# A Fourier-mixing layer with gated MLP: the first DFT block loaded in halves, two scratch tiles for mod's columns, first products regrouped

## The chip, the cores and the metric

The kernel runs on one core of a Trainium2 chip, a single program on core 0. The metric is the device time of one execution in microseconds (us), the median of several runs. The core's engines work side by side, each through its own instructions in program order: TensorE (PE in the profile) multiplies matrices, VectorE (DVE) and ScalarE (ACT) work element by element, GpSimd (POOL) does small arithmetic and issues some DMAs, SyncE (SP) issues the others.

## The reference

The layer has one sequence x of 2048 rows and 512 columns in 32-bit floats. Cut to what matters:

```
mod = (silu(c) @ w_mod).reshape(1, 6, 1, 512)        # sa, ca, ga, sb, cb, gb
h   = layernorm(x) * (1 + ca) + sa
a   = h @ dft_hid_re.T ;  b = h @ dft_hid_im.T       # 512 x 512
x   = x + ga * (dft_seq_re @ a - dft_seq_im @ b)     # 2048 x 2048
h   = layernorm(x) * (1 + cb) + sb
z   = gelu(h @ w_in)                                 # 512 x 1792, two halves z1, z2
g   = w_sp @ layernorm(z2) + b_sp                    # w_sp 2048 x 2048
x   = x + gb * ((z1 * g) @ w_out)                    # 896 x 512
```

## The kernel before, in words

Every product is made in three: a 32-bit operand is split into a high part (a rounded copy, on ScalarE) and a low part (what is left, on VectorE), and TensorE accumulates high by high, high by low and low by high (`matmul3`, lines 84 to 86). The kernel reorders the first layer: it multiplies the sequence DFT with the normalized x first (`gp`, in `mm_a`), then the result with the hidden DFT (`yp`), into which mod's scale `ca` and shift `sa` have been folded. Column 0 of the normalized x is set to 1 for that.

**Chunks.** The sequence DFT is walked in 512 x 512 blocks of the real and the imaginary matrix. `load_block` brings a block to a `stage` tile by four DMAs on SyncE's queue (line 139); there are two such tiles. A block is four chunks. For each chunk n VectorE transposes 32 x 32 squares into `t` (line 147, `prep_hi`), ScalarE rounds it to `ah` (line 170), and VectorE subtracts for `al` (line 179, `prep_lo`). Of every 128 columns of the block, the first 32 make its first chunk, the next 32 its second, and so on. Then TensorE runs the chunk's twelve matmuls: four column groups of x by three products.

**What sets the order.** The loop over n first makes `t` and `ah` for chunk n + 3 and `al` for chunk n + 2, then runs the matmuls of chunk n, then whatever `at(n, ...)` has put on a list for that chunk. In this way an order written out by hand says in which chunk's part of each engine's queue a piece of side work stands. There are four `ah` and three `al` buffers.

**Side work in the first 32 chunks.** The 16 tiles of x are loaded in groups of four (`load_x`), normalized and split into `hh` and `hl`. For the first eight the statistics are made by VectorE (`stats_x`: lines 92 and 94) and a chain of three GpSimd operations (lines 96, 97, 104); for the other eight by two ScalarE passes with an accumulated sum (`sum_x`, `square_x`) and GpSimd operations. `norm_x` applies them on ScalarE (line 108), then sets column 0, for the first four tiles on ScalarE, else on GpSimd. `hi_h` and `lo_h` split.

mod's `ca` (j = 1) and `sa` (j = 0) are wanted as columns. `load_columns` loads a 512 x 512 piece of w_mod, and for each of its four column groups k `weigh_column` transposes squares into a scratch tile `wt` and multiplies by silu(c), both on VectorE, and `sum_column` sums it on ScalarE in the next chunk's list (line 247). `wt` has one buffer. The hidden DFT's rows are turned later into `ht` tiles by `turn_ht`, the first of them in the tile `y` of the pool `rows`, which otherwise belongs to the post-processing of the `yp` products.

**The start.** SyncE loads two x tiles, the first block, two more x tiles, the second block, two x tiles. Meanwhile TensorE multiplies a constant tile (`keep_busy`), seven matmuls of 32-bit operands, shown as two passes each. Within chunk 0 TensorE goes column group by column group: for each, `hh` by `ah`, `hh` by `al`, `hl` by `ah`.

**After chunk 32.** Three more groups of 32 chunks (t = 1, 2, 3) make the next rows. Between their chunks stand the products `yp` with the hidden DFT for rows of the group before (`mm_y`), each followed by a post-processing on VectorE (`post_y`, `norm_y`, `post_h`). After the last chunk of a half (16 chunks) the four accumulators are split into `gh` and `gl` (lines 80, 81). The two later stages, the gated MLP, are not touched by the change.

Of the kernel before, what the change touches and what calls it, by code (L numbers as in the profile page):

```python
# [19 lines left out]
def fnet_gmlp_kernel(  # L20
# [24 lines left out]
    nc = tc.nc  # L45
    S, D = x.shape[1:]
# [11 lines left out]
    def pool(name, side="left", bufs=1):  # L58
        return tc.tile_pool(name=name, bufs=bufs, side=side, reuse_waits="tile")
# [6 lines left out]
    blocks = ctx.enter_context(pool("blocks"))  # L66
# [4 lines left out]
    def bank(k, name):  # L71
        return psum.tile([P, 512], F32, tag=f"bank{k}", bufs=1, name=name)
# [5 lines left out]
    def split(hi, lo, src):  # L78

        nc.scalar.activation(hi, src, AF.Copy)  # L80
        nc.vector.tensor_tensor(lo, src, hi.bitcast(F32), op=ALU.subtract)
# [25 lines left out]
    def apply(dst, src, scale_shift):  # L107
        nc.scalar.activation(dst, src, AF.Identity, bias=scale_shift[1], scale=scale_shift[0])
# [3 lines left out]
    def at(n, f, *a):  # L112
        fill.setdefault(n, []).append((f, a))
# [9 lines left out]
    src = []  # L123
# [4 lines left out]
    N2 = 4 * len(src)  # L128
# [4 lines left out]
    NE = 4 * len(src)  # L133
    stage, T, AH, AL = {}, {}, {}, {}

    def load_block(tile_, a):
        v = a.rearrange("(b j) (a s) -> a j b s", j=32, a=4)
        for q in range(4):
            nc.sync.dma_start(tile_[32 * q:32 * q + 32], v[q])

    def load(b):
        if b < len(src):
            stage[b] = blocks.tile([P, 16, P], F32, tag="stage", bufs=2, name=f"stage{b}")
            load_block(stage[b], src[b])

    def squares(dst, block, k):
        nc.vector.transpose(dst.rearrange("p (b i) -> p b i", i=32), block[:, :, 32 * k:32 * k + 32])  # L147
# [27 lines left out]
    def prep_lo(n):  # L175
        if n >= NE:
            return
        AL[n] = blocks.tile([P, Q], F32R, tag="al", bufs=3, name=f"al{n}")
        nc.vector.tensor_tensor(AL[n], T.pop(n), AH[n].bitcast(F32), op=ALU.subtract)  # L179
# [4 lines left out]
    rows = p2.enter_context(pool("rows", "right"))  # L184
    s1 = ctx.enter_context(ExitStack())
    spool = s1.enter_context(pool("spool", "right"))
# [7 lines left out]
    ones = cpool.tile([P, P], F32, name="ones")  # L194
# [28 lines left out]
    WB, WT, COL = {}, {}, {}  # L223
# [13 lines left out]
        COL[j] = htpool.tile([P, ND], F32, name=f"col{j}")  # L237

    def weigh_column(j, k):
        WT[j, k] = spool.tile([P, D], F32, tag="wt", bufs=1, name=f"wt{j}_{k}")  # L240
        squares(WT[j, k], WB[j], k)
        nc.vector.tensor_tensor(WT[j, k], WT[j, k], WB["c"], op=ALU.mult)

# [11 lines left out]
    def keep_busy(n, k):  # L255

        ps = bank(k, "busyp")
        for _ in range(n):
            nc.tensor.matmul(ps, ones, busy, start=True, stop=True)
# [14 lines left out]
    X, XG, LN, NRM, h_hi, h_lo = {}, {}, {}, {}, {}, {}  # L274

    def load_x(g, ks=range(4)):

        if g not in XG:
            XG[g] = spool.tile([P, 4, D], F32, tag="x", bufs=2, name=f"x{g}")
        k0, k1 = ks[0], ks[-1] + 1  # L280
        v = x.rearrange("(g a k i) d -> g a i k d", g=NQ, a=4, i=32)
        for a in range(4):
            nc.sync.dma_start(XG[g][32 * a:32 * a + 32, k0:k1, :], v[g, a][:, k0:k1, :])
        for k in ks:
            X[4 * g + k] = XG[g][:, k, :]
# [17 lines left out]
        NRM[s] = m[:, 2:3], m[:, 3:4]  # L303

    def norm_x(s):
        if s not in LN:
            LN[s] = spool.tile([P, D], F32, tag="xn", bufs=4, name=f"xn{s}")
        apply(LN[s], X.pop(s), NRM.pop(s))
        if s < 4:
            nc.scalar.activation(LN[s][:, 0:1], ones[:, 0:1], AF.Copy)  # L310
        else:
            nc.gpsimd.memset(LN[s][:, 0:1], 1.0)

    def parts_h(s, t):

        return t[s].rearrange("p k (a i) -> p k a i", i=32), LN[s].rearrange("p (a k i) -> p k a i", a=4, i=32)

    def hi_h(s):
        h_hi[s] = hpool.tile([P, ND, P], F32R, name=f"hh{s}")
        nc.scalar.activation(*parts_h(s, h_hi), AF.Copy)  # L320
# [8 lines left out]
    GP, gt_hi, gt_lo, YP = {}, {}, {}, {}  # L329
# [3 lines left out]
    def mm_a(n):  # L333
        t, r = divmod(n, 8 * NQ)
        j, s = ((r // 4) % 2, r // 8 * 4 + r % 4) if t == 0 else (r // NS, r % NS)
        if s == 0:
            for k in range(ND):
                GP[t, j, k] = bank(4 * j + k if t == 0 else ring[0] % 6, f"gp{t}_{j}_{k}")
                ring[0] += t > 0
        ah, al = AH.pop(n), AL.pop(n)  # L340
        for k in range(ND):
            matmul3(GP[t, j, k], h_hi[s][:, k, :], h_lo[s][:, k, :], ah, al, s == 0, s == NS - 1)
        if s == NS - 1:
            for k in range(ND):
# [261 lines left out]


    load_x(0, range(2))
    load(0)
    load_x(0, range(2, 4))  # L610
    load(1)
    load_x(1, range(2))
    keep_busy(7, 5)
    for s in range(2):
        stats_x(s)
    for s in range(2):
        norm_x(s)
    hi_h(0)
    prep_hi(0)
    lo_h(0)  # L620
    prep_lo(0)
    hi_h(1)
    prep_hi(1)
    stats_x(2)
# [12 lines left out]
    at(9, silu_row)  # L637
    at(4, load_x, 2)
    at(5, load_columns, 1)
    at(8, load_columns, 0)  # L640
    at(12, load_x, 3)
    at(19, load_ht, 0)
    at(28, load_ht, 1)
    for s, n in ((4, 4), (5, 4), (6, 6), (7, 6)):
        at(n, stats_x, s)
        at(n + 1, norm_x, s)
        at(n + 2, hi_h, s)
        at(n + 3, lo_h, s)
    for s, n in zip(range(8, NS), (10, 11, 12, 13, 18, 19, 20, 21)):
        at(n, sum_x, s)  # L650
        at(n + 1, square_x, s)
        at(n + 2, norm_x, s)
        at(n + 3, hi_h, s)
        at(n + 4, lo_h, s)
    for j, ns in ((1, (12, 13, 16, 18)), (0, (19, 20, 21, 23))):
        for k, n in enumerate(ns):
            at(n, weigh_column, j, k)
            at(n + 1, sum_column, j, k)
# [6 lines left out]
    ones_r = htpool.tile([P, P], F32R, name="ones_r")  # L665
    at(24, nc.scalar.activation, ones_r, ones, AF.Copy)
    at(26, change_pools)
    for j, turn, weigh, row, fold, hi in ((0, (24, 25, 26, 27), (29, 29, 30, 30), 25, (34, 34, 35, 36), (38, 35, 36, 37)),
                                          (1, (33, 38, 39, 40), (39, 40, 41, 41), 37, (44, 45, 46, 47), (48, 46, 47, 48))):
        for k in range(ND):  # L670
            at(turn[k], turn_ht, j, k)
            at(weigh[k], weigh_ht, j, k)
            at(fold[k], fold_ht, j, k)
        at(row, scale_w0, j)
        at(row + 1, store_w0, j)
        at(row + 5, load_w0, j)
# [14 lines left out]
    for t in range(NQ):  # L691
        n = 8 * NQ * (t + 1)
        for i in range(4):
            y = N2 - 1 if t == NQ - 1 else (54, 56, 58, 60)[i] if t == 0 else n + (8, 10, 12, 14)[i] if t == 1 else n + 1 + 3 * i
            if i < 2:
                at(y - 4, load_xr, t, i)
            if t == 0:
                at((41, 42, 43, 45)[i], mm_y, t, i, (0,))
                at((42, 43, 44, 46)[i], keep_y, t, i)
            at(y, mm_y, t, i, (0, 1) if t else (1,))  # L700
            if t < NQ - 1:
                at(y + 1, post_y, t, i)
                at(y + 2, norm_y, t, i)
                at(y + 3 if t else 71 + i, post_h, t, i)
                if i < 2:
                    at(y + 2 if t else y + 3, load_xr, t, i + 2)
            else:
                if i > 1:
                    at(N2 - 0.25, prep, N2 + i - 2)
                at(N2 - 0.25, post_y, t, i)  # L710
                at(N2 - 0.25, norm_y, t, i)
                at(N2 - 0.25, post_h, t, i)
                if i < 2:
                    at(N2 - 0.25, load_xr, t, i + 2)
# [59 lines left out]
    for t in range(NQ):  # L774
        n = N4 + NS * (t + 1)
# [14 lines left out]
    t = NQ - 1  # L790
# [61 lines left out]
```

## Time and profile before

| | |
|---|---|
| median of three runs | 1002.48 us (1002.38 to 1003.36) |
| the profiled execution | 1002.74 us |
| its span on the core | 1000.9 us |
| TensorE busy | 989.3 us (99%), 4346 matmul passes |
| VectorE, ScalarE, GpSimd busy | 543.6, 315.1, 142.3 us |
| moved by DMA | 115.08 MB, 115 GB/s in the mean |

The profile is one execution, taken by the hardware profiler. A row of the timeline gives start and duration in us, engine, source line, operation, and output<-inputs by the program's names with shapes; in brackets stands the idle time of the engine before the instruction and what ended it. Matmuls are pipelined, so the time from one start to the next is a matmul's cost, not the shown duration. A row of the waits gives the total in us, the number of times and the longest. A row of a window gives, after the stretch and its length, the busy time and instructions of PE, PEld, DVE, ACT and POOL, TensorE's granted clock as a share of full speed, the DMA engines' mean busy share and GB/s. A row of a DMA queue gives packets, MB, and the share of 16 engines' time.

### The profile page before, as it was taken

The numbers are of one execution on the slowest core, as the hardware profiler recorded it, in microseconds if no ns is written. First come the engines' busy times: TensorE is split into PE (matmuls) and PEld (weight loads), VectorE is DVE, ScalarE is ACT, GpSimd is POOL, SyncE is SP. The second block draws the span as 40 slices with busy tenths as digits, with TensorE's granted clock in tenths as the row PEclk, the third lists the DMA queues.
The fourth block names the chain that finished last, engine by engine and source line by source line (L and its number), as shares of the span: only waits on it lengthen the run. The fifth ranks groups of instructions, "written<-read, shape, count | busy, mean of one in ns | idle before, by whom it ended". The sixth has DMA issues, their size and how long they took to land.

```text
span 1000.9 us, 11701 instructions
## 1 busy us (share of the span) xinstructions
PE 989.3 (99%) x4346; PEld 818.9 (82%) x4346; DVE 543.6 (54%) x830; ACT 315.1 (31%) x513; POOL 142.3 (14%) x282
## 2 busy tenths in 40 slices
PE   8998999999999999999999999999999999999998
PEld 5886888888878888888888998888888888888886
DVE  6768957775566546547433576555332622262315
ACT  4666423232132312222543665431111111111101
POOL 2321000112420122004321111102000200020002
PEclk9999999999999999999999999999999999999999
DMA  9993852666435443556553232435225222522131
GB/s 214 215 198 67 167 138 63 158 166 171 126 103 118 93 109 104 117 127 163 189 204 117 43 80 47 116 69 147 70 63 156 55 64 64 158 64 52 43 137 43
DMA packets 149466, 115.08 MB, mean 115 GB/s; under 512 B 7200, under 2 KB 130080, under 8 KB 149408
## 3 DMA queue, kind: packets, MB, share of 16 engines
q1 hardware_dynamic: 142576, 93.87, 40.7%
q0 software_dynamic: 6304, 20.46, 5.8%
q8 instruction: 34, 0.56, 0.2%
q14 instruction: 24, 0.20, 0.1%
q10 hardware_dynamic: 528, 0.00, 0.0%
HBM read 94.37 MB, written 19.93 MB: 114 GB/s over the span
## 4 chain that ended last, share of the span: by engine, by line
PE 94%; DVE 2%; ACT 1%; DMA 1%; issue 1%; SPq 0%; DVEq 0%; ACTq 0%
PE gp L85 11%; PE gp L86 11%; PE gp L84 10%; PE gw L84 10%; PE gw L86 10%; PE gw L85 10%; PE yp L85 3%; PE yp L84 3%; PE yp L86 3%; PE z2p L85 3%; PE z2p L84 3%; PE z2p L86 3%; PE z1p L84 3%; PE z1p L85 3%; PE z1p L86 3%; PE op L86 2%
## 5 line engine op out<-in xcount | busy, mean ns | idle before, releaser
L170 ACT ACTIVATE ah<-t 128x512 fp32r<-128x512 f32 x224 | 141.5, 632 | 535.6 <-PE gw L86 214.9
L179 DVE TENSOR_TENSOR al<-t,ah 128x512 fp32r<-128x512 f32 x224 | 153.1, 683 | 274.6 <-PE gw L85 143.0
L85 PE MATMUL gp<-al,hh 128*128 128x512 f32 x512 | 201.6, 394 | 4.7 <-DVE al L179 4.7
L84 PE MATMUL gp<-ah,hh 128*128 128x512 f32 x512 | 200.8, 392 | 1.7 <-ACT ah L170 1.7
L86 PE MATMUL gp<-ah,hl 128*128 128x512 f32 x512 | 201.1, 393 | 0.0
L86 PE MATMUL gw<-ah,zl 128*128 128x512 f32 x448 | 174.5, 390 | 0.0
L84 PE MATMUL gw<-ah,zh 128*128 128x512 f32 x448 | 174.5, 389 | 0.0
L85 PE MATMUL gw<-al,zh 128*128 128x512 f32 x448 | 174.5, 389 | 0.0
L147 DVE STREAM_TRANSPOSE t<-stage 128x512 f32<-128x512 f32 x208 | 146.4, 704 | 5.6 <-DMA stage<-in_A_dft_seq_re_dram 2.8
L85 PEld LDWEIGHTS gp<-al,hh 128*128 128x128 f32 x512 | 96.8, 189 | 26.5 <-DVE al L179 6.3
L84 PEld LDWEIGHTS gp<-ah,hh 128*128 128x128 f32 x512 | 97.0, 189 | 23.2 <-ACT ah L170 2.5
L86 PEld LDWEIGHTS gp<-ah,hl 128*128 128x128 f32 x512 | 97.0, 189 | 20.8 <-DVE hl L325 0.4
L86 PEld LDWEIGHTS gw<-ah,zl 128*128 128x128 f32 x448 | 84.1, 188 | 17.5
L85 PEld LDWEIGHTS gw<-al,zh 128*128 128x128 f32 x448 | 84.2, 188 | 17.4
L84 PEld LDWEIGHTS gw<-ah,zh 128*128 128x128 f32 x448 | 84.1, 188 | 17.3
L569 POOL TENSOR_TENSOR u<-u,g 128x512 f32<-128x512 f32 x16 | 21.4, 1340 | 336.1 <-DVE g L567 336.1
L85 PE MATMUL yp<-htl,gh 128*128 128x512 f32 x128 | 51.1, 399 | 0.0
L84 PE MATMUL yp<-hth,gh 128*128 128x512 f32 x128 | 50.5, 394 | 0.0
L86 PE MATMUL yp<-hth,gl 128*128 128x512 f32 x128 | 50.2, 392 | 0.0
L85 PE MATMUL z2p<-wil,ah 128*128 128x448 f32 x128 | 46.8, 366 | 0.0
L84 PE MATMUL z2p<-wih,ah 128*128 128x448 f32 x128 | 46.8, 366 | 0.0
L86 PE MATMUL z2p<-wih,al 128*128 128x448 f32 x128 | 46.8, 366 | 0.0
(125 smaller groups left out, 1132.0 us busy)
## 6 DMA issues: line engine op xcount, KB each, us to landing
stage<-in_A_dft_seq_re_dram SPq DMA_DIRECT2D x64, 256.0 KB, 4.8
stage<-in_A_dft_seq_im_dram SPq DMA_DIRECT2D x64, 256.0 KB, 4.7
stage<-in_B_w_sp_dram SPq DMA_DIRECT2D x64, 256.0 KB, 4.9
stage<-h_d SPq DMA_DIRECT2D x32, 256.0 KB, 4.6
z_d<-z POOLq DMA_DIRECT2D x28, 256.0 KB, 5.9
u<-z_d SPq DMA_DIRECT2D x4, 1792.0 KB, 7.9
wm<-in_w_mod_dram SPq DMA_DIRECT2D x16, 256.0 KB, 5.7
xr<-in_A_x_dram POOLq DMA_DIRECT2D x16, 256.0 KB, 3.0
```

The costliest lines, as they stand in the source:

```text
L84: nc.tensor.matmul(acc, ah, bh, start=first, stop=False)
L85: nc.tensor.matmul(acc, ah, bl, start=False, stop=False)
L86: nc.tensor.matmul(acc, al, bh, start=False, stop=last)
L147: nc.vector.transpose(dst.rearrange("p (b i) -> p b i", i=32), block[:, :, 32 * k:32 * k + 32])
L170: nc.scalar.activation(AH[n], T[n], AF.Copy)
L179: nc.vector.tensor_tensor(AL[n], T.pop(n), AH[n].bitcast(F32), op=ALU.subtract)
L569: eng.tensor_tensor(U[t][:, f, :], U[t][:, f, :], g, op=ALU.mult)
```

## The change

Six edits, all in or around the first 32 chunks but for the last:

- The first block is loaded in two halves of its columns, columns 0 to 63 of every 128 first, which are those of chunks 0 and 1, then the x tiles 2 and 3, then the other half. Each half takes four DMAs.
- `wt` of even column groups uses the tile `y` of `rows`, that of odd groups the tile `wt`.
- In chunks 0 to 3 the twelve matmuls are grouped by product: four `hh` by `ah`, four `hh` by `al`, four `hl` by `ah`. The filler has six matmuls instead of seven.
- Column 0 of the normalized x is set on GpSimd for all tiles, ahead of the normalization, which leaves that column out. x tile 1 is normalized after the first chunk's preparation.
- x tiles 8 and 9 get their statistics from VectorE and GpSimd; the tiles 10 to 15 are taken in other chunks, so are mod's column groups and the turned rows of the hidden DFT, and the last x load stands before the second load of mod's columns.
- For t = 1 the `yp` products stand one chunk earlier.

```
-    def load_block(tile_, a):
+    def load_block(tile_, a, s0=0, s1=P):
         v = a.rearrange("(b j) (a s) -> a j b s", j=32, a=4)
         for q in range(4):
-            nc.sync.dma_start(tile_[32 * q:32 * q + 32], v[q])
+            nc.sync.dma_start(tile_[32 * q:32 * q + 32, :, s0:s1], v[q][:, :, s0:s1])
...
     def weigh_column(j, k):
-        WT[j, k] = spool.tile([P, D], F32, tag="wt", bufs=1, name=f"wt{j}_{k}")
+        pl, tag = (spool, "wt") if k % 2 else (rows, "y")
+        WT[j, k] = pl.tile([P, D], F32, tag=tag, bufs=1, name=f"wt{j}_{k}")
...
-        apply(LN[s], X.pop(s), NRM.pop(s))
-        if s < 4:
-            nc.scalar.activation(LN[s][:, 0:1], ones[:, 0:1], AF.Copy)
-        else:
-            nc.gpsimd.memset(LN[s][:, 0:1], 1.0)
+        nc.gpsimd.memset(LN[s][:, 0:1], 1.0)
+        apply(LN[s][:, 1:], X.pop(s)[:, 1:], NRM.pop(s))
...
+        if n < 4:
+            for a, b in ((h_hi[s], ah), (h_hi[s], al), (h_lo[s], ah)):
+                for k in range(ND):
+                    nc.tensor.matmul(GP[0, 0, k], a[:, k, :], b, start=s == 0 and b is ah and a is h_hi[s], stop=False)
+            return
...
-    load(0)
+    stage[0] = blocks.tile([P, 16, P], F32, tag="stage", bufs=2, name="stage0")
+    load_block(stage[0], src[0], 0, P // 2)
     load_x(0, range(2, 4))
+    load_block(stage[0], src[0], P // 2, P)
...
-    keep_busy(7, 5)
+    keep_busy(6, 5)
...
-    at(8, load_columns, 0)
-    at(12, load_x, 3)
+    at(8, load_x, 3)
+    at(12, load_columns, 0)
...
-    for s, n in zip(range(8, NS), (10, 11, 12, 13, 18, 19, 20, 21)):
+    for s, n in zip(range(10, NS), (11, 12, 15, 16, 18, 19)):
...
-    for j, ns in ((1, (12, 13, 16, 18)), (0, (19, 20, 21, 23))):
+    for j, ns in ((1, (12, 14, 17, 18)), (0, (21, 22, 23, 24))):
...
-            y = ... n + (8, 10, 12, 14)[i] if t == 1 ...
+            y = ... n + (7, 9, 11, 13)[i] if t == 1 ...
```

How the change moves instructions is shown at three places. The first is SyncE's queue at the start: x are the tiles of x, stage_120 the first block, the next stage the second. Before:

```order
L283 DMA x_115<-in_A_x_dram 32x2x512 x4
L139 DMA stage_120<-in_A_dft_seq_re_dram 32x16x128 x4
L283 DMA x_115<-in_A_x_dram 32x2x512 x4
L139 DMA stage_129<-in_A_dft_seq_im_dram 32x16x128 x4
L283 DMA x_134<-in_A_x_dram 32x2x512 x4
```

And now:

```order
L284 DMA x_115<-in_A_x_dram 32x2x512 x4
L139 DMA stage_120<-in_A_dft_seq_re_dram 32x16x64 x4
L284 DMA x_115<-in_A_x_dram 32x2x512 x4
L139 DMA stage_120<-in_A_dft_seq_re_dram 32x16x64 x4
L139 DMA stage_133<-in_A_dft_seq_im_dram 32x16x128 x4
L284 DMA x_138<-in_A_x_dram 32x2x512 x4
```

The first block is two groups of four DMAs, each of 64 instead of 128 columns, with the x tiles 2 and 3 between; four DMAs more stand ahead of the second block.

The second is ScalarE's queue around mod's second set of columns (`wt_0` and `wt_1` of j = 0 are summed into col; `ah` heads each chunk). Before:

```order
L170 ACTIVATE ah_848<-t_846 128x512
L320 ACTIVATE hh_864<-xn_764 128x512
L108 ACTIVATE xn_798<-x_590,sums_799 128x512
L299 ACTIVATE xn_835,sums_836<-x_590,sums_836 128x512
L294 ACTIVATE xn_872,sums_873<-x_590 128x512
L247 ACTIVATE wt_1_840,col_491<-wt_1_840 128x512
L170 ACTIVATE ah_882<-t_880 128x512
```

And now:

```order
L170 ACTIVATE ah_897<-t_895 128x512
L319 ACTIVATE hh_915<-xn_831 128x512
L248 ACTIVATE wt_0_892,col_610<-wt_0_892 128x512
L170 ACTIVATE ah_923<-t_921 128x512
L248 ACTIVATE wt_1_918,col_610<-wt_1_918 128x512
L170 ACTIVATE ah_947<-t_945 128x512
```

Before, five instructions stand between two `ah` with the column's sum as the last; now two or one.

VectorE's queue at the same place. Before:

```order
L147 STREAM_TRANSPOSE t_846<-stage_699 128x512
L179 TENSOR_TENSOR al_850<-t_806,ah_808 128x512
L147 STREAM_TRANSPOSE wt_2_877<-wb_486 128x512
L242 TENSOR_TENSOR wt_2_877<-wt_2_877,crow 128x512
L147 STREAM_TRANSPOSE t_880<-stage_699 128x512
```

And now:

```order
L147 STREAM_TRANSPOSE t_921<-stage_714 128x512
L179 TENSOR_TENSOR al_925<-t_895,ah_897 128x512
L324 TENSOR_TENSOR hl_939<-xn_831,hh_915 128x512
L147 STREAM_TRANSPOSE wt_2_942<-wb_605 128x512
L243 TENSOR_TENSOR wt_2_942<-wt_2_942,crow 128x512
L147 STREAM_TRANSPOSE t_945<-stage_714 128x512
```

The order of a chunk is as before, with an `hl` more in it; `wt_2` now lies in the tile `y`, in which `wt_0` was, while `wt_1` lies in the other.

The third is TensorE's first chunk. Before:

```order
L259 MATMUL busyp<-busy,ones 128x512 x7
L84 MATMUL gp_0_0_233<-ah_175,hh_171 128x512
L85 MATMUL gp_0_0_233<-al_179,hh_171 128x512
L86 MATMUL gp_0_0_233<-ah_175,hl_177 128x512
L84 MATMUL gp_0_1_234<-ah_175,hh_171 128x512
```

And now:

```order
L260 MATMUL busyp<-busy,ones 128x512 x6
L343 MATMUL gp_0_0_236<-ah_175,hh_171 128x512
L343 MATMUL gp_0_1_237<-ah_175,hh_171 128x512
L343 MATMUL gp_0_2_238<-ah_175,hh_171 128x512
L343 MATMUL gp_0_3_239<-ah_175,hh_171 128x512
L343 MATMUL gp_0_0_236<-al_179,hh_171 128x512
```

The first matmul that needs `al` was the second of the chunk and is the fifth.

More of the change, by code (lines that the diff above doesn't have):

```diff
@@ L608, in fnet_gmlp_kernel @@
     load_x(0, range(2))
-    load(0)
+    stage[0] = blocks.tile([P, 16, P], F32, tag="stage", bufs=2, name="stage0")
+    load_block(stage[0], src[0], 0, P // 2)
     load_x(0, range(2, 4))
+    load_block(stage[0], src[0], P // 2, P)
     load(1)
     load_x(1, range(2))
-    keep_busy(7, 5)
+    keep_busy(6, 5)
     for s in range(2):
         stats_x(s)
-    for s in range(2):
-        norm_x(s)
+    norm_x(0)
     hi_h(0)
@@ L621, in fnet_gmlp_kernel @@
     prep_lo(0)
+    norm_x(1)
     hi_h(1)
@@ L639, in fnet_gmlp_kernel @@
     at(5, load_columns, 1)
-    at(8, load_columns, 0)
-    at(12, load_x, 3)
+    at(8, load_x, 3)
+    at(12, load_columns, 0)
     at(19, load_ht, 0)
     at(28, load_ht, 1)
-    for s, n in ((4, 4), (5, 4), (6, 6), (7, 6)):
+    for s, n in ((4, 4), (5, 4), (6, 6), (7, 6), (8, 10), (9, 10)):
+        m = n + (s == 9)
         at(n, stats_x, s)
-        at(n + 1, norm_x, s)
-        at(n + 2, hi_h, s)
-        at(n + 3, lo_h, s)
-    for s, n in zip(range(8, NS), (10, 11, 12, 13, 18, 19, 20, 21)):
+        at(m + 1, norm_x, s)
+        at(m + 2, hi_h, s)
+        at(m + 3, lo_h, s)
+    for s, n in zip(range(10, NS), (11, 12, 15, 16, 18, 19)):
         at(n, sum_x, s)
@@ L667, in fnet_gmlp_kernel @@
     at(26, change_pools)
-    for j, turn, weigh, row, fold, hi in ((0, (24, 25, 26, 27), (29, 29, 30, 30), 25, (34, 34, 35, 36), (38, 35, 36, 37)),
+    for j, turn, weigh, row, fold, hi in ((0, (25, 26, 27, 28), (29, 29, 30, 30), 26, (34, 34, 35, 36), (38, 35, 36, 37)),
                                           (1, (33, 38, 39, 40), (39, 40, 41, 41), 37, (44, 45, 46, 47), (48, 46, 47, 48))):
@@ L693, in fnet_gmlp_kernel @@
         for i in range(4):
-            y = N2 - 1 if t == NQ - 1 else (54, 56, 58, 60)[i] if t == 0 else n + (8, 10, 12, 14)[i] if t == 1 else n + 1 + 3 * i
+            y = N2 - 1 if t == NQ - 1 else (54, 56, 58, 60)[i] if t == 0 else n + (7, 9, 11, 13)[i] if t == 1 else n + 1 + 3 * i
             if i < 2:
```

## The prediction

> **What bounds the kernel now.** I read the page's first part, then TensorE's waits over the whole span, then its timeline around the waits, then what VectorE and ScalarE did there.
>
> ```profile
> span 1000.9 us, 11701 instructions
> PE 989.3 (99%) x4346; PEld 818.9 (82%) x4346; DVE 543.6 (54%) x830; ACT 315.1 (31%) x513; POOL 142.3 (14%) x282
> PE gp L85 <- DVE al L179: 4.7, 4, 3.0
> ```
>
> TensorE is busy 99% of the span and no matmul is added or removed. So only its start, its few waits and its clock can move the end: two places hold nearly all of that. The first is seen in the matmuls (start, duration, and in brackets the wait before):
>
> ```profile
> 24.44 0.39 PE L84 MATMUL gp<-ah,hh 128*128 128x512 f32 x1
> ...
> 76.12 0.39 PE L84 MATMUL gp<-ah,hh 128*128 128x512 f32 x1
> 77.66 0.50 PE L85 MATMUL gp<-al,hh 128*128 128x512 f32 x1 [1.15 <-DVE al L179]
> ...
> 80.29 0.39 PE L84 MATMUL gp<-ah,hh 128*128 128x512 f32 x1
> 83.63 0.66 PE L85 MATMUL gp<-al,hh 128*128 128x512 f32 x1 [2.95 <-DVE al L179]
> ...
> 84.83 0.63 PE L84 MATMUL gp<-ah,hh 128*128 128x512 f32 x1
> 85.25 0.63 PE L85 MATMUL gp<-al,hh 128*128 128x512 f32 x1
> ...
> 88.02 0.39 PE L84 MATMUL gp<-ah,hh 128*128 128x512 f32 x1
> ```
>
> A chunk is twelve matmuls. Chunk 4 starts at 24.44 and chunk 23 at 76.12: 2.72 us a chunk, 0.227 us a matmul, without a gap. At that pace chunk 25 would start at 24.44 + 21 x 2.72 = 81.56; it starts at 88.02. So **6.46 us** are lost in chunks 23 and 24: 4.4 in two waits for `al`, and 2.0 because matmuls after the longer wait start 0.42 us apart, at half pace.
>
> Why `al` was late, on VectorE and then on ScalarE:
>
> ```profile
> DVE wt L147 <- ACT wt L247: 11.9, 5, 3.3
> 76.32 0.71 DVE L147 STREAM_TRANSPOSE t<-stage 128x512 f32<-128x512 f32 x1
> 80.94 0.71 DVE L147 STREAM_TRANSPOSE wt<-wb 128x512 f32<-128x512 f32 x1 [3.34 <-ACT wt L247]
> 81.69 0.69 DVE L242 TENSOR_TENSOR wt<-wt,crow 128x512 f32<-128x512 f32 x1
> 82.30 0.70 DVE L147 STREAM_TRANSPOSE t<-stage 128x512 f32<-128x512 f32 x1
> 82.93 0.65 DVE L179 TENSOR_TENSOR al<-t,ah 128x512 fp32r<-128x512 f32 x1
> 83.50 0.68 DVE L325 TENSOR_TENSOR hl<-xn,hh 128x512 fp32r<-128x512 f32 x1
> 77.12 0.63 ACT L170 ACTIVATE ah<-t 128x512 fp32r<-128x512 f32 x1 [2.57 <-DVE t L147]
> 77.66 0.61 ACT L320 ACTIVATE hh<-xn 128x512 fp32r<-128x512 f32 x1
> 78.18 0.80 ACT L108 ACTIVATE xn<-x,sums 128x512 f32<-128x512 f32 x1
> 78.88 0.71 ACT L299 ACTIVATE xn<-x,sums 128x512 f32<-128x512 f32 x1
> 79.59 0.62 ACT L294 ACTIVATE xn<-x 128x512 f32<-128x512 f32 x1
> 80.20 0.61 ACT L247 ACTIVATE wt<-wt 128x512 f32<-128x512 f32 x1
> ```
>
> It is a ring. With one `wt` tile, VectorE may not transpose the next column group until ScalarE has summed the last one. That sum stands last in the ScalarE queue of the same chunk, behind `ah`, `hh` and three passes over x; and `ah` heads that queue waiting for VectorE's `t`. One round takes from `t` at 76.32 to `t` at 82.30, 5.98 us against TensorE's 2.72. Chunks 19, 20 and 21 each carry such a step, so about 3 x 3.26 = 9.8 us fall behind; `al` has three buffers, two chunks (5.4 us) of lead; 9.8 - 5.4 = 4.4 is what TensorE waited.
>
> **The change part by part.**
>
> *Two scratch tiles.* Column group k now waits for the sum of k-2, which stands in an earlier chunk's ScalarE queue. The ring is open unless the queues themselves are too long. From the starts above VectorE spends 0.63 on `t`, 0.57 on `al`, 0.75 + 0.61 on `wt`, and at most its 0.68 on `hl`. In the new order chunks 21 to 24 hold t, al, wt (2.56), t, al, hl, wt (3.24), the same (3.24), and 2.56: 11.6 us for 10.9 us of matmuls. That costs 0.7 of the 5.4 us lead, and TensorE nothing. ScalarE (`ah` 0.54, `hh` 0.52, `xn` 0.70, square 0.71, sum 0.61) holds at most ah, hh, xn, square, sum, at 3.1, in chunks 12 and 13, and 3.0 in 18 and 19, with 1.8 to 2.3 between them. Moving x tiles 8 and 9 to VectorE's statistics adds two pairs to chunk 10: 1.2 + 2 x 0.83 = 2.9 us there, after a chunk of 1.2, and takes 1.3 a tile off ScalarE. So I take the whole 6.46. The bounds: nothing gained if the ring closes elsewhere, and no more than 6.46, since that is all TensorE lost there. If the lead is gone, each microsecond VectorE is late is a microsecond of TensorE.
>
> The even groups borrow the `y` tile, whose next user is the first turned tile of the hidden DFT, at chunk 25. It waits for the sum in ScalarE's chunk 24, again the earlier queue. Cost: nothing, covered by the lead.
>
> *The start.* SyncE's queue, VectorE, GpSimd, ScalarE, TensorE, a window and a DMA queue:
>
> ```profile
> 2.56 2.02 SPq L139 DMA_DIRECT2D stage<-in_A_dft_seq_re_dram  x4
> 5.38 0.69 DVE L92 BATCH_NORM_STATS2 bstx<-x 128x6 f32<-128x512 f32 x1 [4.00 <-DMA x<-in_A_x_dram]
> 9.92 0.71 DVE L147 STREAM_TRANSPOSE t<-stage 128x512 f32<-128x512 f32 x1 [2.83 <-DMA stage<-in_A_dft_seq_re_dram]
> 8.59 0.26 POOL L104 TENSOR_SCALAR nmrx<-mvx,rsx 128x1 f32<-128x1 f32 x1
> 9.84 0.61 ACT L320 ACTIVATE hh<-xn 128x512 fp32r<-128x512 f32 x1
> 10.66 0.63 ACT L170 ACTIVATE ah<-t 128x512 fp32r<-128x512 f32 x1 [0.21 <-DVE t L147]
> 1.53 8.12 PE L259 MATMUL busyp<-busy,ones 128*128 128x512 f32 x14 [1.53 <-DVE busy L201]
> 11.35 0.49 PE L84 MATMUL gp<-ah,hh 128*128 128x512 f32 x1 [1.70 <-ACT ah L170]
> 12.07 0.77 PE L85 MATMUL gp<-al,hh 128*128 128x512 f32 x1 [0.23 <-DVE al L179]
> 14.53 0.71 DVE L147 STREAM_TRANSPOSE t<-stage 128x512 f32<-128x512 f32 x1
> 13.00:14.00 1.00, 1.00 (x4) 0.74 (x3) 0.97 (x4) 0.30 (x1) 0.48 (x1) 0.50 1.23 247
> 19.89 0.61 ACT L320 ACTIVATE hh<-xn 128x512 fp32r<-128x512 f32 x1
> q10 hardware_dynamic: 528, 0.00, 9.7%
> ```
>
> The block lands 9.92 - 5.38 = 4.54 us after the x tiles: 2048 packets of 512 B over 16 engines, 35.5 ns each. Half a block has as many packets, of 256 B, a size this trace does not hold. From both sides: 17.7 ns by bytes, 35.5 if a packet costs what it did, so 2.27 to 4.54 us. The 4-byte packets of c (last row, a window of 3 us: 0.097 x 48 us / 528) cost 8.8 ns, so a small packet is not dear; the straight line between gives 22 ns, a half in 2.84 us. I take that: `t` of chunk 0 can start at 8.2. Then `hh` is last: its column memset stands behind GpSimd's second chain, which ends at 8.59 + 0.26, so `hh` runs 9.0 to 9.6, `ah` to 10.2, and the first matmul starts near 10.3 (before, 0.69 after `ah` began): 1.05 earlier. Chunk 2 needs the second half: 8.2 + 2.3 (x tiles, 512 KB at the block's rate) + 2.84 = 13.4, when VectorE, also 1.05 earlier, comes to it. The next block lands at 17.9, 1.1 later than by bytes, with three chunks of lead, as for every load behind it (`t` is made three chunks ahead). The four DMAs more take 2.0 us of issuing (2.02 for four), while the data of those ahead, 4.54 us a block, still flows: nothing, and at most 2.0 on loads with that lead.
>
> The regrouped products let four matmuls run before `al` is wanted, so the 0.5 us between 11.35 and 12.07 beyond one matmul goes. From 11.35 to 24.44 is 13.09 = 10.88 (four chunks) + 0.50 + 1.71, the last from the half clock that the window's 0.50 shows. If it stays, chunk 4 starts at 10.3 + 10.88 + 1.71 = 22.9: **1.55 us**. Chunk 3's `hh` ended 5.97 after chunk 2's `t` began (14.53 to 20.50): statistics, GpSimd's chain, `xn`, `ah` and itself stand between. So it ends near 19.4, before TensorE comes at 20.2. Bounds: at 35.5 ns a packet the second half lands at 9.92 + 2.3 + 4.54 = 16.8, chunk 3's `hh` ends at 22.7 and chunk 4 starts at 25.4, 1.0 lost; without the half clock `hh` sets chunk 3 at 19.4 and chunk 4 at 22.1, 2.3 gained.
>
> [...]
>
> *The shift of t = 1's y by one chunk.* One wait of 0.4 us is left, where four `gl` meet the post-processing of a y:
>
> ```profile
> PE gp L85 <- DVE al L179: 0.4, 1, 0.4
> ...
> 284.25 2.76 DVE L81 TENSOR_TENSOR gl<-gp,gh 128x512 fp32r<-128x512 f32 x4 [6.40 <-ACT gh L80]
> 287.52 0.69 DVE L438 TENSOR_TENSOR y<-yp,mod 128x512 f32<-128x512 f32 x1
> ```
>
> The last y now ends a chunk before the `gl`: 0.4 gained, between 0 and 0.4. The x tiles 12 to 15 are loaded four chunks earlier, ahead of block 5 and the second column block in SyncE's queue. Block 5 has as many bytes ahead of it as before, the columns are wanted in chunk 21 only: nothing, under the lead, as for the turned tiles a chunk later. Were the lead gone, block 5 would be late by the rest of its 4.54.
>
> **Sum:** 6.46 + 1.55 + 0.4 = 8.4. The profiled execution took 1002.74 (span 1000.9 and 1.8 around it), so 994.3; the median of the runs lies 0.3 lower, inside what I can tell.
>
> **The rivals.**
>
> *The clock stays up at the start.* Two filler passes of 14 fewer end the filler at 8.5 to 8.8, the gap is 1.5 to 1.8, between the 1.15 that did no harm and the 1.93 that did. Then 2.3 instead of 1.55: 993.5.
>
> *256 B packets cost as much as 512 B.* The start loses 1.0 instead of gaining 1.55: 996.9. Against it: 8.8 ns for 4 B.
>
> *VectorE becomes the bound.* Chunks 21 to 31 hold some 30.5 us of VectorE work (two times four `gl` at 2.76 among it) against 29.9. With a lead already spent one stall like that at 83.63 stays, up to 2.95 + 2.0: 996 to 999.3. Against it: the kernel before went through the same `gl` with little lead and no wait.
>
> *The second tile does not open the ring* (another wait on ScalarE takes its place): only start and y are left, 1000.8. Against it: the two sums lie a whole chunk apart.
>
> *Small packets are dear, and it is slower.* If a 256 B packet cost twice a 512 B one, 71 ns, a half would take 9.1 us: halves at 14.5 and 25.9, chunk 3's `hh` near 31.9, chunk 4 at 34.6 instead of 24.44. That is 10.2 lost against 6.9 gained: 1006. It decides from about 58 ns a packet, where the start's loss equals the 6.9. Against it again: 8.8 ns. [...]
>
> **How the numbers follow.** Forecast 0.50 (994.3); clock stays up 0.18; packets by count 0.10; VectorE the bound 0.07; ring not opened 0.06; dear packets 0.05; something I have not seen 0.04. The range, 992.6 to 998.6, holds the first three and half of the fourth, 0.81. This kernel's measurement tells about 0.2% (2 us) from no change. Faster: the first four and most of the unseen, 0.88; same: 0.07, mostly the ring; slower: 0.05.
>
> **What would show it.** Right: no wait for `al` between chunks 20 and 26; no `wt` transpose waiting over 1 us for ScalarE; first `t` near 8.2, first real matmul near 10.3, chunk 4 near 22.9, chunk 25 57.1 us after it. Wrong: a first `t` at 9.9 or later (packets), a wait for `al` with VectorE busy throughout (bound), with VectorE idle (a ring again).

## The result, and the profile after

The changed kernel takes **993.07 us** (992.93 to 993.16, four runs), the kernel before on the same chip 1002.43 (1000.97 to 1003.36, four runs): a ratio of 0.9908, 95% interval 0.9891 to 0.9925, so 0.9% faster. The forecast was 994.3. Three executions on record, one each of the kernel before, of this kernel and of the kernel with column 0 set first (below), took 1415 to 1663 us at a mean granted clock of 0.56 to 0.66 and are left out of all figures here.

The changed kernel's page, its first rows and the chain that ended last:

```profile
span 991.3 us, 11711 instructions
PE 984.6 (99%) x4344; PEld 816.0 (82%) x4344; DVE 545.5 (55%) x834; ACT 312.0 (31%) x501; POOL 145.9 (15%) x284
PE 98%; SPq 1%; DMA 0%; DVE 0%; ACT 0%; issue 0%
```

The profiled execution took 993.14, 9.60 less than the one before (1002.74). TensorE is still busy for 99% of the span and holds 98% of the chain. Its busy time fell too, by 4.7 us, of which the shorter filler is 0.5 (8.12 to 7.59): much of what went was not idleness but work at half pace.

All of TensorE's waits in the changed kernel (line, releaser: us in total, times, longest):

```profile
PE busyp L260 <- DVE busy L201: 1.5, 1, 1.5
PE gp L343 <- ACT ah L170: 1.0, 1, 1.0
PE gp L343 <- ACT hh L319: 0.3, 1, 0.3
```

No wait for `al` is left anywhere; before there were four, 4.7 us. Where the 9.6 us went is read from TensorE's timeline (start, duration, wait before):

```profile
1.53 7.59 PE L260 MATMUL busyp<-busy,ones 128*128 128x512 f32 x12 [1.53 <-DVE busy L201]
10.16 1.21 PE L343 MATMUL gp<-ah,hh 128*128 128x512 f32 x4 [1.04 <-ACT ah L170]
11.21 1.09 PE L343 MATMUL gp<-al,hh 128*128 128x512 f32 x4
12.14 1.08 PE L343 MATMUL gp<-ah,hl 128*128 128x512 f32 x4
...
14.87 1.07 PE L343 MATMUL gp<-ah,hl 128*128 128x512 f32 x4
16.23 1.19 PE L343 MATMUL gp<-ah,hh 128*128 128x512 f32 x4 [0.29 <-ACT hh L319]
17.26 1.08 PE L343 MATMUL gp<-al,hh 128*128 128x512 f32 x4
...
21.82 0.39 PE L84 MATMUL gp<-ah,hh 128*128 128x512 f32 x1
...
78.94 0.39 PE L84 MATMUL gp<-ah,hh 128*128 128x512 f32 x1
```

- **Start.** Chunk 4 begins at 21.82 instead of 24.44: 2.62 us.
- **Ring.** Chunk 25 begins at 78.94, 57.12 us behind chunk 4: 21 chunks at 2.72 without a gap. Before it took 63.58 (24.44 to 88.02): 6.46 us.
- **y.** The wait of 0.4 us near 284 is gone.

That makes 9.5 of the 9.6; the last 0.1 is spread.

VectorE at the place of the ring in the changed kernel:

```profile
71.43 0.69 DVE L324 TENSOR_TENSOR hl<-xn,hh 128x512 fp32r<-128x512 f32 x1
72.03 0.70 DVE L147 STREAM_TRANSPOSE wt<-wb 128x512 f32<-128x512 f32 x1
72.77 0.69 DVE L243 TENSOR_TENSOR wt<-wt,crow 128x512 f32<-128x512 f32 x1
73.38 0.71 DVE L147 STREAM_TRANSPOSE t<-stage 128x512 f32<-128x512 f32 x1
...
75.17 0.70 DVE L147 STREAM_TRANSPOSE wt<-wb 128x512 f32<-128x512 f32 x1
```

Two transposes into `wt`, 3.14 us apart, with no wait in front of either; before, the one at 80.94 stood 3.34 us. What VectorE waits for between 40 and 120 us is now mostly TensorE, which means that it is ahead (the `al` of a later chunk waits for a matmul to release its buffer):

```profile
DVE al L179 <- PE gp L85: 5.7, 8, 1.2
```

The start on VectorE and ScalarE:

```profile
5.42 0.69 DVE L92 BATCH_NORM_STATS2 bstx<-x 128x6 f32<-128x512 f32 x1 [4.03 <-DMA x<-in_A_x_dram]
7.65 0.71 DVE L147 STREAM_TRANSPOSE t<-stage 128x512 f32<-128x512 f32 x1 [0.53 <-DMA stage<-in_A_dft_seq_re_dram]
8.96 0.63 ACT L319 ACTIVATE hh<-xn 128x512 fp32r<-128x512 f32 x1 [0.50 <-POOL xn L310]
9.50 0.61 ACT L170 ACTIVATE ah<-t 128x512 fp32r<-128x512 f32 x1
```

The half block lands 7.65 - 5.42 = 2.23 us after the x tiles (4.54 for the whole block before), and `hh` is then the last thing missing, held by GpSimd's column memset, as forecast. And the granted clock in the slice that read 0.50 before:

```profile
13.00:14.00 1.00, 1.00 (x6) 0.81 (x6) 1.00 (x2) 0.00 (x0) 0.88 (x1) 1.00 1.25 259
```

(The three last figures of such a row are the clock, the DMA share and GB/s.) It stays at 1.00 in every slice of a microsecond from 3 to 20 us. That is what the forecast did not expect.

### The profile page after: what moved, and what is told of

The parts are those of the page before. It is cut to its first block, busy times and chain, and to the rows that moved or that the text cites. A ratio compares the mean times of both kernels' runs of the same rounds, so it can differ in the third digit from the quotient of the medians.

```text
span 991.3 us, 11711 instructions
## 1 busy us (share of the span) xinstructions
PE 984.6 (99%) x4344; PEld 816.0 (82%) x4344; DVE 545.5 (55%) x834; ACT 312.0 (31%) x501; POOL 145.9 (15%) x284
## 4 chain that ended last, share of the span: by engine, by line
PE 98%; SPq 1%; DMA 0%; DVE 0%; ACT 0%; issue 0%
PE gp L84 11%; PE gp L85 11%; PE gp L86 11%; PE gw L84 10%; PE gw L85 10%; PE gw L86 10%; PE yp L85 3%; PE yp L84 3%; PE yp L86 3%; PE z2p L85 3%; PE z2p L86 3%; PE z2p L84 3%; PE z1p L84 3%; PE z1p L85 3%; PE z1p L86 3%; PE op L84 2%
## 5 line engine op out<-in xcount | busy, mean ns | idle before, releaser
L84 PE MATMUL gp<-ah,hh 128*128 128x512 f32 x496 | 193.3, 390 | 0.0
L85 PE MATMUL gp<-al,hh 128*128 128x512 f32 x496 | 193.3, 390 | 0.0
L86 PE MATMUL gp<-ah,hl 128*128 128x512 f32 x496 | 193.2, 389 | 0.0
L84 PEld LDWEIGHTS gp<-ah,hh 128*128 128x128 f32 x496 | 93.1, 188 | 19.8
L86 PEld LDWEIGHTS gp<-ah,hl 128*128 128x128 f32 x496 | 93.1, 188 | 19.8
L85 PEld LDWEIGHTS gp<-al,hh 128*128 128x128 f32 x496 | 93.1, 188 | 19.4
L84 PEld LDWEIGHTS gw<-ah,zh 128*128 128x128 f32 x448 | 84.1, 188 | 17.4
```

Of the source, the lines that this page charges most:

```text
L84: nc.tensor.matmul(acc, ah, bh, start=first, stop=False)
L85: nc.tensor.matmul(acc, ah, bl, start=False, stop=False)
L86: nc.tensor.matmul(acc, al, bh, start=False, stop=last)
```

## The experiments

Each kernel was timed in four or five runs beside the kernel before; the ratios are to that. The theory going in: the ring cost 6.46 and a second tile opens it; the start gave 2.62 because the clock was not halved there. The rival for the first is that the new order of the side work did it; for the second, that bytes or packets of the load, or the regrouped products, did it.

### The second tile alone

The kernel before, with one edit:

```
-        WT[j, k] = spool.tile([P, D], F32, tag="wt", bufs=1, ...)
+        pl, tag = (spool, "wt") if k % 2 else (rows, "y")
+        WT[j, k] = pl.tile([P, D], F32, tag=tag, bufs=1, ...)
```

> The kernel before with only the second scratch tile; order, start and everything else as before. Theory (the ring through one tile delayed al): VectorE's waits of 11.9 us for the column sums fall below 1 us, TensorE does not wait in chunks 20 to 26, 6.5 us are saved: about 996.0. Rival (the new order of the side work did it, not the tile): at least half of the 6.5 us stays, 999 or more.

Measured: 996.28 (995.47 to 996.75), ratio 0.9935 (0.992 to 0.995), before 1002.93: 6.6 us. TensorE's waits in it:

```profile
PE gp L84 <- ACT ah L170: 1.8, 1, 1.8
...
PE gp L85 <- DVE al L179: 0.6, 2, 0.4
```

The 0.6 are the start's 0.23 and the y's 0.4; between chunks 4 and 25 there is nothing. The ring is opened by the tile alone, in the old order, with its five instructions between two `ah`. Of the runs timed side by side, one of each kernel had a mean granted clock of 1.000; between those two the difference is 5.5 us (1000.94 and 995.47), so about 1 us of the 6.6 seems to be half pace that goes with the stall.

### The new order with one tile

The changed kernel with that edit undone.

> The changed kernel with one scratch tile again, its order kept. If the ring costs what stands in ScalarE's queue of the same chunk, it is short here (in chunks 22 to 24 ah, at most one hh, the sum): a round of 3.2 to 3.7 us against 2.72, some 2.5 us behind over three chunks, less than the 5.4 us of lead, so TensorE does not wait: about 993.1. Rival (one tile alone brings the stall back): 6.4 us are lost again, about 999.5.

Measured: 993.45 (993.41 to 994.91), ratio 0.9911 (0.9896 to 0.9926). The profiled execution is the one of 994.91. VectorE's waits in it between 40 and 120 us:

```profile
DVE wt L147 <- ACT wt L247: 5.8, 5, 3.1
DVE t L147 <- DMA stage<-in_A_dft_seq_re_dram: 2.5, 1, 2.5
```

and the one marked wait that reached TensorE there:

```profile
85.55 0.50 PE L85 MATMUL gp<-al,hh 128*128 128x512 f32 x1 [0.38 <-DVE al L179]
```

So, with the new order, one tile loses only 0.4 us in the medians: VectorE still waits 5.8 us for sums, but the lead of `al` pays for it, since in chunks 22 to 24 only `hh` or nothing stands between `ah` and the sum in ScalarE's queue. In this execution a block also came 2.5 us late, out of the same lead, and small gaps of 0.1 to 0.5 reached TensorE, some 1.5 us in all. The two edits are two cures for one wait: the tile alone is worth 6.6 us, the order by subtraction (6.46 less 0.4) some 6, though it was not run by itself on the kernel before. Both together leave the lead whole for something else. The expectation held for three runs to 0.4 us, not for the fourth.

### The whole first block ahead of x's next tiles

The changed kernel with the first block loaded as before:

```
-    stage[0] = blocks.tile(...)
-    load_block(stage[0], src[0], 0, P // 2)
+    load(0)
     load_x(0, range(2, 4))
-    load_block(stage[0], src[0], P // 2, P)
```

> The changed kernel with the first block loaded whole, before the x tiles 2 and 3. The first transpose waits until 9.9 and the first real matmul starts near 11.1, 1.0 later. If the length of TensorE's idle gap sets the clock (2.0 us here, 1.04 with halves, 1.93 before), the matmuls then run at half pace for 3.4 us: about 995. Rival (the clock stays up): only the 1.0 to 1.2 us of the later start, 994.2.

Measured: 994.27 (993.98 to 995.36), ratio 0.9918 (0.9903 to 0.9933): the halves are worth 1.2 us. TensorE's first real matmul, and the clock behind it:

```profile
11.65 1.20 PE L343 MATMUL gp<-ah,hh 128*128 128x512 f32 x4 [2.08 <-ACT ah L170]
```

```profile
13.00:14.00 1.00, 1.00 (x6) 0.84 (x5) 0.97 (x3) 0.62 (x2) 0.17 (x1) 1.00 1.24 235
```

A gap of 2.08 us, longer than the 1.70 + 0.23 of the kernel before, and the clock stays. The half clock that I expected came in one run of four (995.36, mean granted clock 0.998); the rival's 994.2 held for the others.

### The products of chunks 0 to 3 by column group

```
-        if n < 4:
+        if n < 0:
```

> The changed kernel with the products of chunks 0 to 3 by column group again. The second matmul waits for al (about 10.9 against a start at 10.16), so 0.5 us are lost in chunk 0 and some tenths in chunks 1 and 2, less the 0.3 us that chunk 2 waits for hh anyway: 993.4 to 993.8. Rival (the grouping is hidden by chunk 2's wait): 993.1.

Measured: 993.37 (993.23 to 994.53), ratio 0.9908 (0.9894 to 0.9922). The profiled execution is the slowest of them:

```profile
10.01 0.50 PE L84 MATMUL gp<-ah,hh 128*128 128x512 f32 x1 [1.51 <-ACT ah L170]
10.82 0.51 PE L85 MATMUL gp<-al,hh 128*128 128x512 f32 x1 [0.31 <-DVE al L179]
```

The wait for `al` returns, 0.31 plus what stands around it, 0.58 beyond a matmul's 0.227 between the two starts. The median is only 0.3 higher. The rest probably disappears in chunk 2's wait for `hh`: this execution has none, but it is also the one at half clock, and no trace at full clock shows it. Here the clock did halve, after 1.51 + 0.31:

```profile
12.00:13.00 1.00, 1.00 (x4) 0.72 (x4) 1.00 (x3) 0.05 (x1) 0.65 (x2) 0.50 1.25 209
```

### The filler shorter: five passes, and three

The changed kernel with `keep_busy(5, 5)`, and with `keep_busy(3, 5)`, for 6: only the gap in front of the first real matmul grows.

> The changed kernel with five filler matmuls instead of six, so that the filler ends near 8.26 and TensorE idles 1.9 us, about as long as in the kernel before (1.70 + 0.23), with the first real matmul where it was (10.16). If the gap's length halves the clock: 1.7 us lost, less the 0.3 us that chunk 2 waits anyway: about 994.5. Rival (the gap does not decide, the halves and the regrouping alone did): 993.1.

Measured: 993.08 (993.0 to 993.9), ratio 0.9907 (0.989 to 0.9923). The gap was 2.03 us, and in the profiled execution the clock stayed; one run of four (993.90) was slower at a lower mean clock (0.998). So the rival's 993.1 was measured, not the theory's 994.5:

```profile
10.05 1.21 PE L343 MATMUL gp<-ah,hh 128*128 128x512 f32 x4 [2.03 <-ACT ah L170]
```

> The changed kernel with three filler matmuls instead of six: the filler ends near 6.6 or earlier, TensorE idles some 3.5 us before the first real matmul at 10.16. Theory (the clock halves when TensorE is busy for less than about half of a window of some 3.4 us, and where the windows lie differs from execution to execution): with such a gap a window of that kind is always there, so every run loses 1.4 to 1.8 us: 994.4 to 994.9, with the granted clock at 0.5 for some 3.4 us. Rival (the clock at the start has nothing to do with the filler): 993.1.

Measured: 993.77 (993.62 to 995.03), ratio 0.9914 (0.9898 to 0.9931). Every run lost, by 0.6 to 2.0 us:

```profile
10.05 2.08 PE L343 MATMUL gp<-ah,hh 128*128 128x512 f32 x4 [3.44 <-ACT ah L170]
```

```profile
9.00:10.00 1.00, 0.00 (x0) 0.00 (x0) 0.49 (x1) 1.00 (x3) 0.00 (x0) 0.76 1.16 252
10.00:11.00 1.00, 0.95 (x2) 0.83 (x3) 1.00 (x3) 0.91 (x2) 0.00 (x0) 0.50 1.05 227
...
12.00:13.00 1.00, 1.00 (x4) 0.81 (x3) 0.96 (x4) 0.09 (x1) 0.61 (x2) 0.53 1.18 212
13.00:14.00 1.00, 1.00 (x5) 0.80 (x5) 1.00 (x3) 0.00 (x0) 0.90 (x2) 1.00 1.25 250
```

With 3.44 us idle the clock is halved, and four matmuls take 2.08 instead of 1.21. The loss is smaller than expected: the half clock began at about 9.5 (0.76 in that slice), 0.5 us of it lay in the idle gap, and 2.9 us at half pace cost about 1.45. From the first matmul to chunk 4 (22.40) this execution loses 1.47 against matmuls at pace, the changed kernel 0.78, mostly to chunk 2's wait for `hh` (worked out further below), which is gone here; so 0.7 was left. The filler's effect shows in the clock alone: with five passes (a gap of 2.03 us in the profiled execution) it is enough in three runs of four, with three passes (3.44 us) in none. The theory's "about half" is an estimate of mine from the busy shares in the last section: up to 0.47 where the clock halved, from 0.61 where it did not.

### The first half block in two quarters

```
-    load_block(stage[0], src[0], 0, P // 2)
+    load_block(stage[0], src[0], 0, P // 4)
+    load_block(stage[0], src[0], P // 4, P // 2)
```

> The changed kernel with the first half of the first block loaded as two quarters, so with 128 B packets. If packets cost by bytes, the first quarter is there before VectorE has finished the statistics: the first transpose starts at 7.1 without a wait, but hh is still last, and four more DMAs hold SyncE's queue 2 us longer, so x tiles 2 and 3 and the second half come later: 993.3 to 993.9. If a 128 B packet costs what a 256 B one did, the first transpose starts near 7.65 and the half needs twice as long: 994 or more.

Measured: 993.4 (993.15 to 993.68), ratio 0.9907 (0.9892 to 0.9921). VectorE, then SyncE's queue:

```profile
5.06 0.69 DVE L92 BATCH_NORM_STATS2 bstx<-x 128x6 f32<-128x512 f32 x1 [3.67 <-DMA x<-in_A_x_dram]
...
6.76 0.71 DVE L147 STREAM_TRANSPOSE t<-stage 128x512 f32<-128x512 f32 x1
...
13.95 0.71 DVE L147 STREAM_TRANSPOSE t<-stage 128x512 f32<-128x512 f32 x1 [0.48 <-DMA stage<-in_A_dft_seq_re_dram]
```

```profile
2.56 4.14 SPq L139 DMA_DIRECT2D stage<-in_A_dft_seq_re_dram  x8
```

The first transpose did not wait at all; the x tiles had landed at 5.06, so 128 packets of 128 B per engine landed at most 1.70 us later, 13.3 ns each; from 5 to 8 us, 3015 packets, all but 6 under 512 B, took 82.8% of the 16 engines' time, 13.2 ns each. That is nothing gained, since `hh` is last, and eight DMAs at 0.52 us of issuing put x's next tiles and the second half later: the wait at 13.95 is new. In the window from 5 to 8 us the load moved 129 GB/s:

```profile
5.00:8.00 3.00, 3.00 (x9) 1.21 (x7) 2.35 (x5) 0.71 (x1) 1.58 (x5) 1.00 0.83 129
```

against, in the changed kernel,

```profile
5.00:8.00 3.00, 3.00 (x7) 1.31 (x6) 1.99 (x5) 0.35 (x1) 1.23 (x5) 1.00 0.98 251
```

A quarter's DMA carries 64 KB, and one every 0.52 us is 126 GB/s: the issuing explains the rate. Whether 128 B packets could flow faster is not told by this run; but the engines were 0.83 busy for 129 GB/s, against 0.98 for 251, so by these two rows a byte kept them busy 1.6 times as long.

### t = 1's y back by one chunk

`n + (7, 9, 11, 13)[i]` back to `n + (8, 10, 12, 14)[i]` in the changed kernel.

> The changed kernel with the y products of t = 1 where they were. Theory (the last y's post-processing met the gl): the wait for al near 284 less 9 us comes back, 0.4 us: 993.5. Rival (the wait hung on something else): 993.1, no wait.

Measured: 993.66 (993.54 to 993.79), ratio 0.9911 (0.9897 to 0.9925), 0.6 over the changed kernel. The wait is back where it was:

```profile
282.39 0.50 PE L85 MATMUL gp<-al,hh 128*128 128x512 f32 x1 [0.39 <-DVE al L179]
```

With the restart behind it (0.77 from the matmul ahead at 281.62, for 0.227 at pace) the place costs 0.54.

### The changed kernel again, and two steps further

> The changed kernel itself, as the measure for differences of under 1 us on this chip: 993.1.

Measured: 993.03 (992.95 to 993.05), ratio 0.9905 (0.9891 to 0.9919): 993.07 is reproduced. Beside it ran the changed kernel with the first four column memsets at the very start of GpSimd's queue, so that `hh` no longer waits behind GpSimd's second chain:

```
+    for s in range(4):
+        LN[s] = spool.tile([P, D], F32, tag="xn", bufs=4, ...)
+        nc.gpsimd.memset(LN[s][:, 0:1], 1.0)
     load_x(0, range(2))
```

> The changed kernel with column 0 of the first four normalized tiles set on GpSimd at the very start, before the statistics. The first hh waits 0.50 us for that column now; without it hh, ah, the first matmul (9.66) and all behind it come 0.5 us earlier, and chunk 2's wait of 0.3 us shrinks: 992.5. Rival (the DMA of x tiles 2 and 3 or of the second half sets chunk 2): 993.1.

Measured: 992.53 (992.47 to 992.58), ratio 0.99 (0.9884 to 0.9916), and once more:

> The kernel with column 0 set at the very start once more, as the measure for the next one on the same chip: 992.5.

992.67 (992.62 to 992.73), ratio 0.9899 (0.9885 to 0.9914). No run of either overlaps the changed kernel's: 0.4 to 0.5 us better. The first matmul and chunk 2's, the second time:

```profile
9.56 1.20 PE L344 MATMUL gp<-ah,hh 128*128 128x512 f32 x4 [0.45 <-ACT ah L170]
...
15.71 0.50 PE L344 MATMUL gp<-ah,hh 128*128 128x512 f32 x1 [0.42 <-ACT hh L320]
```

The first matmul comes 0.60 earlier, of which 0.14 is x landing earlier in this execution (the first normalization starts at 7.51 for 7.65); the wait in chunk 2 for `hh` grows. The last kernel tries that one too, with `prep_hi(2)` ahead of `norm_x(2)`, so that `ah` isn't behind `xn` on ScalarE.

> The kernel with column 0 set at the start, and ah of chunk 2 ahead of the normalization of x tile 2 in ScalarE's queue. ScalarE waits there for GpSimd's chain while t is there already; with ah out of the way hh comes 0.2 to 0.3 us earlier, and chunk 2 waits 0.4 us for hh: 992.3. Rival (t of chunk 2 is no earlier than the chain): 992.5.

Measured: 992.55 (992.45 to 992.67), ratio 0.9898 (0.9883 to 0.9913), 0.1 under its neighbour. ScalarE in it,

```profile
13.63 0.63 ACT L170 ACTIVATE ah<-t 128x512 fp32r<-128x512 f32 x1 [1.97 <-DVE t L147]
14.16 0.80 ACT L108 ACTIVATE xn<-x,nmrx,rsx 128x511 f32<-128x511 f32 x1
15.00 0.63 ACT L320 ACTIVATE hh<-xn 128x512 fp32r<-128x512 f32 x1
```

and in its neighbour,

```profile
13.80 0.82 ACT L108 ACTIVATE xn<-x,nmrx,rsx 128x511 f32<-128x511 f32 x1 [2.13 <-POOL nmrx L104]
14.52 0.61 ACT L170 ACTIVATE ah<-t 128x512 fp32r<-128x512 f32 x1
15.04 0.61 ACT L320 ACTIVATE hh<-xn 128x512 fp32r<-128x512 f32 x1
```

In both, the three stand back to back, and `hh` comes last. `ah` is released by `t` at 13.63, only 0.17 before `xn` by GpSimd at 13.80, so starting with it moves `hh` from 15.04 to 15.00. A miss: the order of two instructions moves little where both of their inputs come at nearly the same time.

## Why the prediction was right, and where it was off

**The ring: right to its size.** 6.46 forecast, 6.46 in the trace, and 57.12 us from chunk 4 to chunk 25 for 57.1. The tile alone gives it (6.6 in the medians). That the size is exact owes something to the execution that was profiled, with 2.0 us of half pace in the stall; without a halving, by the one pair of runs above, the stall is worth about 5.5. What the prediction did not see is that the new order would nearly have given it with one tile: I put the gain down to the tile and used the order only to show that the queues were short enough.

**The start: 1.55 forecast, 2.62 measured, and this is the step that failed.** The term that failed is the half clock behind the first matmul, which the prediction left standing. The terms:

- *First matmul 1.05 earlier*: 1.19 (10.16 for 11.35). The load step behind it was mis-sized. A 256 B packet was put at 22 ns on a line between 512 B and 4 B; measured like the 35.5, from the landing of the x tiles, it took 2.23 us / 128 = 17.4 ns, what its bytes cost (17.7). `t` began at 7.65 and not 8.2. It moved nothing, as the prediction had `hh` last anyway, at 9.0 to 9.6; it ran from 8.96 to 9.59.
- *0.50 for the regrouped products*: the trace has four matmuls ahead of `al` without a wait. Taken out alone it costs 0.3 in the medians; that a later wait swallows the rest is likely, not shown.
- *1.71 of half clock, "if it stays"*: it did not. From 10.16 to 21.82 are 11.66, which is 10.88 for four chunks and 0.78, where before it was 13.09 = 10.88 + 2.21. The 0.78 is nearly all waits: 0.45 in front of chunk 2's `hh` (16.23, at pace it would be 15.78), about 0.13 in the restart behind each of the two waits. I had taken the same clock loss over because 1.70 + 0.23 had halved it and the new gap was to be 1.5 to 1.8. The gap was 1.04, since the first matmul came earlier and the filler ended at 9.12, not at 8.5 to 8.8. That is partly chance: the filler's end moves from execution to execution, and with the same six matmuls and the first real one at 10.0 to 10.1 the gap was 0.18 in one profiled execution (one tile) and 1.51 in another (products by group).

So the rival "the clock stays up" (2.3 us, chunk 4 at 22.1, 993.5) was what happened, with chunk 4 at 21.82. Its own bound was a little off too: chunk 3 began at 19.08, not held by `hh` until 19.4; the wait for `hh` was in chunk 2. I gave that rival 0.18 against 0.50: I went by one gap of the profile that halved the clock and one that did not, and took the length of the gap for the cause. The runs show that this isn't enough.

**y: right.** 0.4 forecast, 0.39 in the trace, 0.6 between the medians when undone.

**The other rivals.** Packets by count or dear ones (996.9, 1006) are excluded by 2.23 us for a half. VectorE as the bound (996 to 999.3) is excluded by its waits for TensorE and by the absence of any for `al`. The ring closing elsewhere (1000.8) is excluded by the rows above. Of the marks that I named, the first matmul (10.16 for 10.3) and the absence of `al` waits fell right; the first `t` came at 7.65, earlier than 8.2; chunk 4 near 22.9 fell wrong, by the clock. A slip that costs nothing: "no matmul is added or removed" leaves out the filler's, two passes fewer (4344 for 4346).

## What to carry to other kernels

When one scratch buffer passes between two in-order queues, find its producer's and its consumer's places in the queues: if the consumer's turn stands behind work that waits for the producer, each use costs a whole round, and the stalls show later, when the lead of another buffer is used up. A second buffer or a shorter queue in front of the consumer cures it (here the tile alone was worth 6.6 us, and the new order with one tile lost 0.4), so try them apart before crediting either. Where a stall stands at the start, ask what a gap does to the granted clock, and read it as a chance and not as a fixed price: one run of four lost to it with the filler of five, one of four with the whole first block, all four with the filler of three.

## What the runs showed of the hardware

**The clock halves for 3.4 us at a time, and whether it does differs between executions of one kernel.** Each run has a mean granted clock of its own, and it sorts the times (one such halving is 0.0017 of a span of 1000 us):

| kernel | runs at 0.999 to 1.000 | runs at 0.994 to 0.998 |
|---|---|---|
| before | 1000.94 to 1001.12 | 1001.90 to 1003.94 |
| second tile alone | 995.47 | 996.26 to 996.75 |
| whole first block | 993.98 to 994.30 | 995.36 |
| products by group | 993.23 to 993.41 | 994.53 |
| filler of five | 993.00 to 993.11 | 993.90 |
| filler of three | none | 993.62 to 995.03 |
| changed kernel (both times) | 992.93 to 993.16 | none |

So of the 9.4 us between the medians, the kernel before has up to 1.4 from its clock (1002.43 against some 1001.0 without a halving; 18 of its 22 runs beside the experiments are in the right column), and the changed kernel never pays it in eight runs. In the slices quoted of the kernel with the filler of three, the half clock runs from about 9.52 (0.76 in that slice) to 12.94 (0.53): 3.42 us. The four other halvings in the profiled executions, two of them in the kernel before, last 3.41 to 3.42 us too.

The length of the gap does not decide: 1.51 + 0.31 (products by group), 1.70 + 0.23 (before) and 1.84 + 0.23 (second tile alone) halved the clock in the profiled executions; 2.03 (filler of five) and 2.08 (whole block) did not. An estimate of mine, worked out from the profiled executions alone, lays windows as long as a halving (3.41 us) end to end, from a moment that differs between executions, and has the clock fall behind a window in which TensorE was busy for less than about half. The kernel before agrees with it within one execution:

```profile
12.00:13.00 1.00, 0.93 (x2) 0.81 (x3) 1.00 (x3) 0.33 (x1) 0.00 (x0) 0.57 1.24 208
83.00:84.00 1.00, 0.37 (x1) 0.19 (x1) 1.00 (x3) 0.90 (x2) 0.00 (x0) 0.91 0.00 0
```

From the clock in such slices, its halvings begin at 12.13 and at 83.81, 71.68 us apart, 21.02 times the 3.41 us that a halving lasts in it. At the start, the filler's passes go from 0.85 to 0.43 us apart at a different moment in each execution (4.7 to 7.6 us; the clock's rows read 1.00 there, so this step is read from the pace). If windows of 3.41 us are laid from that moment, the share of the window with the gap (with the larger part of it, where two share it) in which the profile has TensorE busy is 0.44 (before), 0.39 (second tile alone) and 0.47 (by group), all halved at the window's end, and 0.61 (whole block), 0.66 (filler of five) and 0.77 (changed kernel), none halved. With the filler of three it is 0.15, and in the kernel before's long wait for `al` 0.13, both halved; in the window before that one, which holds the wait of 1.15 us, it is 0.80, not halved. These are few executions, and no run tested the estimate by itself. A gap of 1.04 us leaves at least 0.69 of such a window busy wherever it lies (1 - 1.04 / 3.41), above all the shares that halved the clock here; one of 2 us leaves 0.41 to 0.71, which holds shares of both kinds. As the changed kernel's gap itself differs between executions, eight runs without a halving are a count and not a guarantee.

**Packets of 256 B cost no more by the byte than those of 512 B in the load of the first block.** From the landing of the x tiles to that of the load they come to 17.4 ns each, against 35.5 for 512 B and at most 13.3 for 128 B. The DMA engines' own time agrees: from 5.00 to 5.42 us, when the changed kernel moved none but packets under 512 B (461 packets, 121.2% of 16 engines' time, 272 GB/s), it was 17.7 ns a packet; in the same stretch of the kernel before, nearly all of 512 B (209 packets, 124.2%, 249 GB/s), it was 39.9. In the window from 5 to 8 us the DMA engines moved 251 GB/s in the changed kernel, about half of it in 256 B packets and the rest in the larger ones of the x tiles. What small pieces did cost is SyncE's time, about 0.5 us for each DMA (2.02 for the half's four, 4.14 for the eight of the two quarters).
